# Holding the loads of later batches until the DMA transposes of a batch are done, and issuing the first of those transposes two pairs earlier, in a fused attention and feed-forward kernel

## The chip, the cores and the metric

The kernel runs on one core of one Trainium2 chip. The metric is device time of one execution in microseconds (us). A run is called fast when it is within 1.5% of the fastest of its kernel, and only fast runs are compared. The quoted time is their median. The profile is a trace of one execution; its span is some 2 us shorter than the device time of the same execution (453.2 against 454.95 us for the kernel before), so spans are compared with spans and times with times. In the profile PE is TensorE, PEld its weight loads, DVE VectorE, ACT ScalarE, POOL GpSimd, and SP SyncE; a "q" behind a name means that the line is a DMA issue of that engine.

## The reference

Grouped-query attention (8 batches, 16 query heads, 4 key/value heads, sequence 384, head size 64), and then a feed-forward on the attention's output:

```python
scores = scale * np.matmul(q, k.transpose(0, 1, 3, 2))     # k, v repeated 4 times over heads
attn = softmax(scores)
x = (attn @ v).transpose(0, 2, 1, 3).reshape(B * S, H * D) # 3072 x 1024
h = np.maximum(x @ w_in, 0.0)                              # w_in 1024 x 2048
return (h * h @ w_out).astype(np.float32)                  # w_out 2048 x 1024
```

All inputs and the output are float32 in memory; the kernel computes in bf16.

## The kernel before

A pair is two query heads of one batch: 8 pairs per batch, 64 in all, numbered n. For each pair TensorE computes scores into PSUM, ScalarE takes the exp, TensorE multiplies by v ("attend", one pair behind), and SyncE sends the result through a DMA transpose into `xT` (`put_x`). Between these pieces TensorE works on the feed-forward of the batch before (`fill`), in program order. The feed-forward of batch b may not start before `ready` says so, and it needs `xT` of all 8 pairs of its batch. It begins with the products with `w_in` (the "up matmuls", `f_ps<-xT,w_in_sb` in the profile), in steps of four: the first step of a tile needs `xT` of the batch's first four pairs, the second that of the last four.

q, k and v of a batch are loaded by GpSimd, with a cast from float32 to bf16, into staging buffers (`q_st`, `k_st`, `v_st`). `prepare(b)` then has SyncE transpose k and q by DMA into `kT` and `qT`. Batches 0 and 1 are transposed on TensorE; batch 2 is the first to use `prepare`.

```python
def dup_all_k(b):
    ...                                   # DVE: k_dup <- k_st
    if b + 2 < B:
        load_k(b + 2)

def prepare(b):
    dup_all_k(b)
    R.add("sync", ... dma_start_transpose(kT <- k_dup) ...)
    for part in range(2):
        R.add("sync", ... dma_start_transpose(half of qT <- q_st) ...)
    if b + 2 < B:
        load_q(b + 2)

def prepare_v(b):
    ...                                   # DVE: v_aug <- v_st
    if b + 2 < B and b >= 1:
        load_v(b + 2)
...
for n in range(NPB, NP + 1):              # NPB = 8 pairs of a batch
    per = PER_PAIR[n // NPB]              # ns of feed-forward per pair: 3200 for 8..15, then 5000
    if n < NP:
        scores_pair(n)
    fill(per * 0.4)
    if n > NPB:
        attend(n - 1, 0)
    fill(per * 0.2)
    if n > NPB:
        attend(n - 1, 1)
        put_x(n - 1)
    if n % NPB == (6 if n < 2 * NPB else 4) and n // NPB + 1 < B:
        prepare(n // NPB + 1)
    if n % NPB == 7 and n // NPB + 1 < B:
        prepare_v(n // NPB + 1)
    fill(per * 0.4)
    ready[0] = max(0, n // NPB - 1)
```

Before this loop, the first burst of loads is queued: weights, batches 1 and 2, and, early in the program, q, k and v of batch 3.

The softmax here doesn't subtract the row's maximum and nothing guards it: scores larger than these inputs give would overflow.

Of the kernel before, what the change touches and what calls it, by code (L numbers as in the profile page):

```python
# [106 lines left out]
def bass_gqa_attention__then__ffn_squared_relu_kernel(  # L107
# [11 lines left out]
    B, H, S, D = 8, 16, 384, 64  # L119
# [4 lines left out]
    NPB = H // 2  # L124
# [5 lines left out]
    R = Recorder(nc)  # L130

    def sb(name, shape, dt=bf16):
        return nc.alloc_sbuf_tensor(name, shape, dt)
# [6 lines left out]
    q_st = [sb(f"q_st{i}", [128, H, NJ * D]) for i in range(NST)]  # L140
    k_st = [sb(f"k_st{i}", [128, HKV, NJ, D]) for i in range(NKS)]
    v_st = [sb(f"v_st{i}", [128, HKV, NJ, D]) for i in range(NST)]
# [19 lines left out]
    sc_flat = sc_ps.ap().rearrange("p b c -> p (b c)")  # L162


    def load_k(b):
        st = b % NKS
        R.add("gpsimd", lambda g: g.dma_start(  # L167
            k_st[st].ap().rearrange("p g j d -> p g (j d)"),
            k[b].rearrange("g (p j) d -> p g (j d)", j=NJ)),
            writes=[("k_st", st)], dma=f"k{st}")  # L170

    def load_v(b):
        st = b % NST
        R.add("gpsimd", lambda g: g.dma_start(  # L174
            v_st[st].ap().rearrange("p g j d -> p g (j d)"),
            v[b].rearrange("g (p j) d -> p g (j d)", j=NJ)),
            writes=[("v_st", st)], dma=f"v{st}")

    def load_q(b):
        st = b % NST  # L180
        R.add("gpsimd", lambda g: g.dma_start(  # L181
            q_st[st][:, :, :], q[b].rearrange("h (p j) d -> p h (j d)", j=NJ)),
            writes=[("q_st", st, c) for c in range(NPB)], dma=f"q{st}")

    NWB = 8
    WC = FF // NWB
# [19 lines left out]
    def first_q(c0, c1):  # L206
# [9 lines left out]
        writes=["v_f"], dma="vf")  # L216
# [22 lines left out]
    for c in range(2, NPB):  # L239
        cast_q(c)  # L240
        load_w_in(c - 1)
    load_w_in(7)
    load_k(1)
    load_q(1)
    load_v(1)
    for i in range(2):
        load_w_out(i)
    load_k(2)
    load_q(2)
    load_v(2)  # L250


# [8 lines left out]
    def idle_on_sc(count):  # L261
        def mm(pe):
            for _ in range(count):
                m = pe.matmul(sc_ps[:, 3, 0:256], warm[:, 0:128], warm[:, 0:256])
            return m

        R.add("tensor", mm, reads=["warm"], writes=[("sc", 3)])
# [44 lines left out]
    def dup_all_k(b):  # L312
        src = k_st[b % NKS].ap().rearrange("p g j d -> p (g j) d").unsqueeze(2)
        R.add("vector", lambda e: e.tensor_copy(  # L314
            k_dup[b % 2][:, :, :, :], src.to_broadcast([128, HKV * NJ, 2, D])),
            reads=[("k_st", b % NKS)], writes=[("k_dup", b % 2, g) for g in range(HKV)])
        if b + 2 < B:
            load_k(b + 2)

    def prepare(b):  # L320
        st = b % NST
        dup_all_k(b)
        R.add("sync", lambda e: e.dma_start_transpose(  # L323
            kT[b % 2].ap().rearrange("p g (j c) -> p (g j) c", j=NJ),
            k_dup[b % 2].ap().rearrange("p a x d -> p (a x d)")),
            reads=[("k_dup", b % 2, g) for g in range(HKV)],
            writes=[("kT", b % 2, g) for g in range(HKV)], dma=f"kt{b % 2}")
        for part in range(2):
            cs = range(4 * part, 4 * part + 4)
            R.add("sync", lambda e, cs=cs: e.dma_start_transpose(  # L330
                qT[b % 2][:, cs.start:cs.stop, :].rearrange("p h (t c) -> p (h t) c", t=NJ),
                q_st[st][:, 2 * cs.start:2 * cs.stop, :].rearrange("p h e -> p (h e)")),
                reads=[("q_st", st, c) for c in cs], writes=[("qT", b % 2, c) for c in cs],
                dma=f"qt{b % 2}_{part}")
        if b + 2 < B:
            load_q(b + 2)

    def prepare_v(b):
        R.add("vector", lambda e: e.tensor_copy(
            v_aug[b % 2][:, :, 0:D], v_st[b % NST].ap().rearrange("p g j d -> p (g j) d")),  # L340
            reads=[("v_st", b % NST)], writes=[("v_aug", b % 2)])
        if b + 2 < B and b >= 1:
            load_v(b + 2)

    def operands(p):
# [19 lines left out]
    def scores_pair(p):  # L365
        kt, qt, keys = operands(p)
        half = NJ * S

        def piece(pe, x, j, c0, c1):
            at = x * half + j * S  # L370
            rows = slice(64 * x, 64 * x + 64)
            return pe.matmul(sc_flat[:, at + c0:at + c1], kt[rows, j * 128:(j + 1) * 128], qt[rows, c0:c1])  # L372

        def run(pieces, writes, after=()):
            def mm(pe):
                for pc in pieces:
                    m = piece(pe, *pc)
                return m

            return R.add("tensor", mm, reads=keys, writes=writes, after=after)  # L380

        sc_keys = [("sc", i) for i in range(5)]
        first = run([(0, 2, 256, 384)], sc_keys)
        run([(1, 1, 0, 384), (0, 0, 0, 384), (1, 2, 0, 128), (0, 1, 0, 128), (1, 2, 128, 384),
             (0, 1, 128, 384)], sc_keys)
        run([(1, 0, 0, 384), (0, 2, 0, 256)], sc_keys, after=[first])
        src = sc_flat[:, 0:2 * half].rearrange("p (x a c) -> p x a c", x=2, c=128)
        dst = expT[p % NEX].ap().rearrange("p j (t x c) -> p x (j t) c", x=2, t=NJ)
        R.add("scalar", lambda e: e.activation(dst, src, AF.Exp, scale=0.125),  # L389
              reads=sc_keys, writes=[("expT", p % NEX, j) for j in range(NJ)])  # L390

    def attend(p, s, alone=False):
        b, g = p // NPB, (p % NPB) // 2
        acc, acc_key = (po_alt, ("sc", 1)) if alone and s == 1 else (po_v, "po")

        def av(pe):
            for i in range(NJ):
                f = NJ * s + i
                for j in range(NJ):
                    m = pe.matmul(acc[:, i, s, :], expT[p % NEX][:, j, f * 128:(f + 1) * 128],  # L400
                                  v_aug[b % 2][:, g * NJ + j, :], start=(j == 0), stop=(j == NJ - 1))
            return m

        R.add("tensor", av, reads=[("expT", p % NEX, j) for j in range(NJ)] +
              [("v_aug", b % 2), ("v_one", b % 2)], writes=[acc_key])
        if alone or s == 1:
            ss = slice(s, s + 1) if alone else slice(0, 2)
            w = ss.stop - ss.start
            rinv_v = rinv[p % 2][:, :, ss].unsqueeze(3)
            R.add("vector", lambda e: e.reciprocal(rinv_v, acc[:, :, ss, D:D + 1]),  # L410
                  reads=[acc_key], writes=[("rinv", p % 2)])
            rb = rinv_v.to_broadcast([128, NJ, w, D])
            R.add("vector", lambda e: e.tensor_tensor(o_sb[p % NO][:, :, ss, :], acc[:, :, ss, 0:D], rb, ALU.mult),  # L413
                  reads=[acc_key, ("rinv", p % 2)], writes=[("o_sb", p % NO, s)])

    def put_x(p):
        b, c = p // NPB, p % NPB
        R.add("sync", lambda e: e.dma_start_transpose(
            xT[b % NXT][:, c, :].rearrange("p (i c) -> p i c", i=NJ),
            o_sb[p % NO].ap().rearrange("p i s d -> p (i s d)")),  # L420
            reads=[("o_sb", p % NO, x) for x in range(2)], writes=[("xT", b % NXT, c)], dma=f"xt{p % 8}")
# [71 lines left out]
    def fill(ns):  # L493
        credit[0] += ns
        while credit[0] > 0:
            t = next(ffn, 0)
            if not t:
                credit[0] = 0.0
                return
            credit[0] -= t  # L500
# [32 lines left out]
    idle_on_sc(2)  # L533
    first_oT(NPB - 1, (0,))
    idle_on_sc(3)
    load_q(3)
    fill(6000.0)
    dup_all_k(1)
    fill(1500.0)
    for g in range(HKV):  # L540
        first_kT(g, 1)
        fill(700.0)
    prepare_v(1)
    for c in range(NPB):
        first_qT(c, 1)
        fill(500.0)
    for n in range(NPB, NP + 1):
        per = PER_PAIR[n // NPB]
# [6 lines that stand above are left out]
        if n > NPB:  # L555
            attend(n - 1, 1)
            put_x(n - 1)
        if n % NPB == (6 if n < 2 * NPB else 4) and n // NPB + 1 < B:
            prepare(n // NPB + 1)
        if n % NPB == 7 and n // NPB + 1 < B:  # L560
            prepare_v(n // NPB + 1)
        fill(per * 0.4)
        ready[0] = max(0, n // NPB - 1)
# [32 lines left out]
```

## Time and profile before

| | before |
|---|---|
| time, median of 4 fast runs | 454.34 us (453.99 to 454.69) |
| span of the profile | 453.2 us |
| TensorE busy | 430.9 us |
| longest wait of TensorE | 11.3 us, on the DMA transpose into qT |
| mean granted TensorE clock | 0.981 |

The page of the kernel before: busy time of TensorE, then its busy tenths, the granted clock in tenths and the DMA engines' busy tenths in 40 slices of 11.3 us.

```profile
span 453.2 us, 8216 instructions
...
PE 430.9 (95%) x3591; PEld 241.1 (53%) x3626; DVE 165.7 (37%) x357; ACT 198.8 (44%) x209; POOL 33.2 (7%) x48
...
PE   8989999269999999999999999999999999999997
...
PEclk9999999759999999999999999999999999999999
DMA  9999999960099207921296206121432210220011
```

TensorE is busy nearly throughout, but not in the eighth and ninth slice, 79 to 102 us. There it is busy for 2 and 6 tenths, its clock falls, and the DMA engines are busy for 9 and 6 tenths. The timeline of that stretch (start, duration, engine, line, operation, output<-inputs, count, then the idle time before it and what ended it):

```profile
78.01 0.74 POOL L167 DMA_DIRECT2D k_st<-in_k_dram  x1 [38.71 <-DVE k_dup L314]
78.07 0.67 PE L372 MATMUL sc_ps<-qT,kT 64*128 64x128 bf16 x9
78.49 1.52 SPq L323 DMA_TRANSPOSE kT<-k_dup  x1
78.74 1.17 POOL L181 DMA_DIRECT2D q_st<-in_q_dram  x1
...
79.88 0.78 POOL L174 DMA_DIRECT2D v_st<-in_v_dram  x1
80.05 11.20 SPq L330 DMA_TRANSPOSE qT<-q_st  x2
...
80.97 1.02 PE L447 MATMUL f_ps<-w_out_sb,h2T 128*128 128x512 bf16 x4
...
93.34 1.14 PE L372 MATMUL sc_ps<-qT,kT 64*128 64x128 bf16 x9 [11.35 <-DMA qT<-q_st]
...
97.75 4.68 PE L429 MATMUL f_ps<-xT,w_in_sb 128*128 128x384 bf16 x16
```

The scores of pair 15 start at 78.07, those of pair 16, the first of batch 2, at 93.34. TensorE is idle for 11.35 us because the transposes into `kT` and `qT` were issued at 78.49 and 80.05, in the same two microseconds as the loads of batch 4. The DMA view says how long each took from issue to landing (KB as bf16 in SBUF, us):

```profile
q_st<-in_q_dram POOLq DMA_DIRECT2D x1, 768.0 KB, 13.4
k_st<-in_k_dram POOLq DMA_DIRECT2D x1, 192.0 KB, 5.9
v_st<-in_v_dram POOLq DMA_DIRECT2D x1, 192.0 KB, 13.9
...
kT<-k_dup SPq DMA_TRANSPOSE x1, 8.4
qT<-q_st SPq DMA_TRANSPOSE x1, 13.2
```

13.2 us is the first half of `qT`; the second took 9.6 us. The same transposes of batch 6, which has no load beside it, took 3.9 us (`kT`) and 4.8 and 3.9 us (the halves of `qT`); those of batch 7, without a load too, took 5.6, 5.4 and 4.9 us.

The idle time has a tail. The windows view (stretch, its length, busy us of PE, PEld, DVE, ACT and POOL, then the granted clock, the busy share of the DMA engines and GB/s):

```profile
82.00:84.00 2.00, 0.00 (x0) 0.00 (x0) 0.83 (x2) 0.00 (x0) 0.00 (x0) 1.00 0.47 46
84.00:86.00 2.00, 0.00 (x0) 0.00 (x0) 0.00 (x0) 0.00 (x0) 0.00 (x0) 0.65 1.50 223
...
98.00:100.00 2.00, 2.00 (x8) 0.90 (x7) 0.00 (x0) 1.95 (x1) 0.00 (x0) 0.50 0.03 5
100.00:102.00 2.00, 2.00 (x9) 1.03 (x8) 0.56 (x1) 0.52 (x1) 0.00 (x0) 0.58 0.00 0
```

The clock record of the trace has half clock from 84.60 to 101.67 us, 17.07 us. Between 93.34 and 101.67 TensorE has work again and does it slowly: one pair's scores take 1.14 us where pair 15's took 0.67.

### The profile page before, as it was taken

The numbers are of one execution on the slowest core, as the hardware profiler recorded it, in microseconds if no ns is written. First come the engines' busy times: TensorE is split into PE (matmuls) and PEld (weight loads), VectorE is DVE, ScalarE is ACT, GpSimd is POOL, SyncE is SP. The second block draws the span as 40 slices with busy tenths as digits, with TensorE's granted clock in tenths as the row PEclk, the third lists the DMA queues.
The fourth block names the chain that finished last, engine by engine and source line by source line (L and its number), as shares of the span: only waits on it lengthen the run. The fifth ranks groups of instructions, "written<-read, shape, count | busy, mean of one in ns | idle before, by whom it ended". The sixth has DMA issues, their size and how long they took to land.

```text
span 453.2 us, 8216 instructions
## 1 busy us (share of the span) xinstructions
PE 430.9 (95%) x3591; PEld 241.1 (53%) x3626; DVE 165.7 (37%) x357; ACT 198.8 (44%) x209; POOL 33.2 (7%) x48
## 2 busy tenths in 40 slices
PE   8989999269999999999999999999999999999997
PEld 4556554136655565456655565446654566545543
DVE  3546323114422444324433344234432344214411
ACT  4943654144643465336642466325653266203400
POOL 5931001100010002000200000000000000000000
PEclk9999999759999999999999999999999999999999
DMA  9999999960099207921296206121432210220011
GB/s 245 195 196 204 208 203 164 150 123 19 10 163 174 65 20 99 199 73 42 34 148 165 65 20 124 64 65 56 65 76 88 66 33 17 65 80 23 1 69 70
DMA packets 95939, 44.70 MB, mean 99 GB/s; under 512 B 74400, under 2 KB 89760, under 8 KB 95904
## 3 DMA queue, kind: packets, MB, share of 16 engines
q0 software_dynamic: 34288, 16.65, 28.3%
q1 hardware_dynamic: 59504, 25.96, 25.1%
q10 hardware_dynamic: 2112, 1.57, 1.1%
q8 instruction: 28, 0.46, 0.4%
q14 instruction: 7, 0.06, 0.0%
HBM read 35.65 MB, written 12.58 MB: 106 GB/s over the span
## 4 chain that ended last, share of the span: by engine, by line
PE 91%; DMA 3%; DVE 2%; ACT 2%; issue 1%; SPq 0%
PE f_ps L429 38%; PE f_ps L447 36%; PE po L400 8%; PE sc_ps L372 7%; DMA qT<-q_st 3%; ACT expT L362 1%; PE f_ps L256 1%; PE sc_ps L286 1%; PE sc_ps L356 1%; ACT expT L389 0%; DVE o_sb L413 0%; DVE qT L291 0%; SPq L323 0%; DVE hr L436 0%; DVE y_sb L456 0%
## 5 line engine op out<-in xcount | busy, mean ns | idle before, releaser
L429 PE MATMUL f_ps<-xT,w_in_sb 128*128 128x384 bf16 x1024 | 184.6, 329 | 1.2 <-DVE xT L291 0.7
L447 PE MATMUL f_ps<-w_out_sb,h2T 128*128 128x512 bf16 x733 | 176.0, 379 | 2.0 <-issue 0.2
L389 ACT ACTIVATE expT<-sc_ps 128x2304 bf16<-128x2304 f32 x56 | 116.8, 2085 | 108.8 <-PE sc_ps L372 107.5
L429 PEld LDWEIGHTS f_ps<-xT,w_in_sb 128*128 128x128 bf16 x1024 | 94.1, 98 | 64.2 <-issue 8.0
L438 ACT ACTIVATE h2T<-hr 128x384 bf16<-128x384 f32 x128 | 66.6, 521 | 115.5 <-DVE hr L436 114.2
L447 PEld LDWEIGHTS f_ps<-w_out_sb,h2T 128*128 128x128 bf16 x768 | 68.8, 97 | 75.9 <-issue 5.7
L436 DVE TENSOR_SCALAR hr<-f_ps 128x384 f32<-128x384 f32 x128 | 71.2, 557 | 102.7 <-PE f_ps L429 102.7
L456 DVE COPY y_sb<-f_ps 128x512 f32<-128x512 f32 x48 | 33.2, 691 | 110.6 <-PE f_ps L447 110.2
L400 PEld LDWEIGHTS po<-v_aug,expT 128*128 128x128 bf16 x1143 | 52.1, 98 | 23.8 <-ACT expT L362 2.6
L400 PE MATMUL po<-v_aug,expT 128*128 128x65 bf16 x1143 | 56.9, 194 | 1.3 <-ACT expT L362 0.9
L372 PE MATMUL sc_ps<-qT,kT 64*128 64x128 bf16 (+2 forms) x504 | 38.1, 276 | 12.8 <-DMA qT<-q_st 11.3
L372 PEld LDWEIGHTS sc_ps<-qT,kT 64*128 64x128 bf16 x504 | 21.1, 95 | 34.4 <-issue 28.0
L413 DVE TENSOR_TENSOR o_sb<-po,rinv 128x384 bf16<-128x384 f32 x64 | 35.5, 554 | 2.2
L410 DVE RECIPROCAL rinv<-po 128x6 f32<-128x6 f32 x64 | 12.2, 191 | 55.4 <-PE po L400 55.4
L362 ACT ACTIVATE expT<-sc_ps 128x768 bf16<-128x768 f32 x24 | 18.4, 810 | 4.4 <-PE sc_ps L356 3.6
L167 POOL DMA_DIRECT2D k_st<-in_k_dram x7 | 5.3, 761 | 187.8 <-DVE k_dup L314 187.8
L256 PE MATMUL f_ps<-warm 128*128 128x256 bf16 x29 | 7.2, 360 | 1.5 <-DVE warm L221 1.1
L356 PE MATMUL sc_ps<-qT,kT 64*128 64x384 bf16 x48 | 8.1, 332 | 0.3 <-ACT expT L362 0.2
L181 POOL DMA_DIRECT2D q_st<-in_q_dram x7 | 8.3, 1190 | 0.0
L189 POOL DMA_DIRECT2D w_in_sb<-in_moe_w_in_dram x8 | 7.1, 893 | 0.0
L256 PEld LDWEIGHTS f_ps<-warm 128*128 128x128 bf16 x29 | 3.3, 124 | 4.3 <-DVE qT L291 1.5
L174 POOL DMA_DIRECT2D v_st<-in_v_dram x7 | 5.5, 786 | 0.0
(40 smaller groups left out, 52.3 us busy)
## 6 DMA issues: line engine op xcount, KB each, us to landing
out_dram<-y_sb SPq DMA_DIRECT2D x48, 256.0 KB, 2.0
q_st<-in_q_dram POOLq DMA_DIRECT2D x7, 768.0 KB, 13.4
w_in_sb<-in_moe_w_in_dram POOLq DMA_DIRECT2D x8, 512.0 KB, 10.2
w_out_sb<-in_moe_w_out_dram POOLq DMA_DIRECT2D x2, 2048.0 KB, 32.6
k_st<-in_k_dram POOLq DMA_DIRECT2D x7, 192.0 KB, 5.9
v_st<-in_v_dram POOLq DMA_DIRECT2D x7, 192.0 KB, 13.9
xT<-o_sb SPq DMA_TRANSPOSE x56, 2.3
q_f<-in_q_dram ACTq DMA_DIRECT2D x1, 768.0 KB, 8.6
```

The source lines that it names most:

```text
L256: m = pe.matmul(f_ps[1][:, 0:256], warm[:, 0:128], warm[:, 0:256])
L356: m = pe.matmul(sc_ps[:, 2 * u + x, 0:S], kt[rows, j * 128:(j + 1) * 128], qt[rows, :])
L362: R.add("scalar", lambda e: e.activation(dst, src, AF.Exp, scale=0.125), reads=[("sc", 2 * u), ("sc", 2 * u + 1)], writes=[("expT", p % NE ...
L372: return pe.matmul(sc_flat[:, at + c0:at + c1], kt[rows, j * 128:(j + 1) * 128], qt[rows, c0:c1])
L389: R.add("scalar", lambda e: e.activation(dst, src, AF.Exp, scale=0.125), reads=sc_keys, writes=[("expT", p % NEX, j) for j in range(NJ)])
L400: m = pe.matmul(acc[:, i, s, :], expT[p % NEX][:, j, f * 128:(f + 1) * 128], v_aug[b % 2][:, g * NJ + j, :], start=(j == 0), stop=(j == NJ ...
L413: R.add("vector", lambda e: e.tensor_tensor(o_sb[p % NO][:, :, ss, :], acc[:, :, ss, 0:D], rb, ALU.mult), reads=[acc_key, ("rinv", p % 2)] ...
L429: m = pe.matmul(f_ps[u][:, 0:S], w_in_sb[:, kc, c * 128:(c + 1) * 128], xT[b % NXT][:, kc, :], start=(kc == 0), stop=(kc == NKC - 1))
L436: R.add("vector", lambda e: e.tensor_scalar_max(hr[r][:, :], f_ps[u][:, 0:S], 0.0), reads=[("f_ps", u)], writes=[("hr", r)])
L438: R.add("scalar", lambda e: e.activation(h2T[b % 2][:, c, :], hr[r][:, :], AF.Square), reads=[("hr", r)], writes=[("h2T", b % 2, c)])
L447: m = pe.matmul(f_ps[u][:, :], h2T[b % 2][:, c, i * 128:(i + 1) * 128], w_out_sb[:, c, jj * 512:(jj + 1) * 512], start=(c == 0), stop=(c = ...
L456: R.add("vector", lambda e: e.tensor_copy(y_sb[yb][:, :], f_ps[u][:, :]), reads=[("f_ps", u)], writes=[("y", yb)])
```

## The change

The intent is to keep loads and transposes apart. The loads of batches 3 and on are released by the landing of the last `qT` transpose of batch b-1 or b-2, not by program order (v of batch 4 and later only stands behind the released loads in GpSimd's queue); and the transposes of batch 2 are issued at pair 12 instead of 14, to leave them time before pair 16. The core of the diff:

```diff
-    def load_k(b):
+    def load_k(b, after=()):
...                                        # the same for load_v and load_q; after= adds waits
@@ dup_all_k
-        if b + 2 < B:
-            load_k(b + 2)
@@ prepare
-            R.add("sync", lambda e, cs=cs: e.dma_start_transpose(
+            last = R.add("sync", lambda e, cs=cs: e.dma_start_transpose(
...
-        if b + 2 < B:
-            load_q(b + 2)
+        for ahead in range(b + 1 if b == 2 else b + 2, min(b + 3, B)):
+            load_k(ahead, [last])
+            load_q(ahead, [last])
+            if b == 2 and ahead == 3:
+                load_v(ahead, [last])
@@ prepare_v
-        if b + 2 < B and b >= 1:
+        if b + 2 < B and b >= 2:
             load_v(b + 2)
@@ before the loop
-    load_q(3)
@@ loop
-        if n % NPB == (6 if n < 2 * NPB else 4) and n // NPB + 1 < B:
+        if n % NPB == 4 and n // NPB + 1 < B:
```

More of the change, by code (lines that the diff above doesn't have):

```diff
@@ L169, in load_k, with load_v @@
             k[b].rearrange("g (p j) d -> p g (j d)", j=NJ)),
-            writes=[("k_st", st)], dma=f"k{st}")
-    def load_v(b):
+            writes=[("k_st", st)], dma=f"k{st}", after=after)
+    def load_v(b, after=()):
         st = b % NST
@@ L176, in load_v, with load_q @@
             v[b].rearrange("g (p j) d -> p g (j d)", j=NJ)),
-            writes=[("v_st", st)], dma=f"v{st}")
-    def load_q(b):
+            writes=[("v_st", st)], dma=f"v{st}", after=after)
+    def load_q(b, after=()):
         st = b % NST
@@ L182, in load_q @@
             q_st[st][:, :, :], q[b].rearrange("h (p j) d -> p h (j d)", j=NJ)),
-            writes=[("q_st", st, c) for c in range(NPB)], dma=f"q{st}")
+            writes=[("q_st", st, c) for c in range(NPB)], dma=f"q{st}", after=after)
     NWB = 8
```

## The prediction

> What bounds the kernel now. The page shows TensorE busy 430.9 of 453.2 us; the chain that ended last is 91% TensorE. After the start-up it loses little except in one place. The timeline of 60 to 100 us shows its last matmul of pair 15 ending near 82.0 and the scores of pair 16 (first of batch 2) starting at 93.34, 11.35 us idle, released by the DMA transpose into qT; the chain holds the same step, 13.20 us from 80.05. kT was issued at 78.49, qT at 80.05 (landing after 13.2 and 11.4 us, DMA view), while the loads of batch 4 were issued at 78.0 to 79.9. Batch 6 prepared with no load beside it: kT 3.9 us, qT 4.8 and 4.3 us.
>
> The stall costs more than its length. The windows show the granted clock at 1.00 in 82 to 84, 0.65 in 84 to 86 and 0.50 until about 101.7, some 17.1 us: five of the 3413 ns windows that the Trainium skill gives (TensorE: Matmul & The Clock Gate, Part 1). Work from 93.3 to 102.3 ran cold: scores 1.14 us instead of 0.66, sixteen up matmuls 4.5 instead of 2.6. Estimated loss 2.8 us. Removable: 11.3 + 2.8 = 14.1 us, all on the chain; that alone would give 440.3.
>
> What moves. Batch 3's loads no longer end the first burst: q(3) landed at 72.8, k(3) 74.5, v(3) 76.2. q(2), ahead of them, landed at 65.1 and k(2) at 59.4, so prepare(2) at pair 12 should find its inputs: kT issued near 70.4, qT at 72 to 75.7, landing near 78. Pair 16's scores start near 82: the wait disappears. Work hardly changes.
>
> What it adds. Landing near 78 releases k3, q3, v3, k4, q4, then v4: 2.36 MB in SBUF. The software queue moved 1.95 MB in the 12 us of 54 to 66, so this lasts about 14.5 us, from 79.5 to 94. Feed-forward of batch 1 starts in pair 17, and its second step needs xT of pair 15, issued only near 84.6. Transposes of xT issued under load at 55 to 70 landed in 6.1 to 7.7 us, without load in 2.3. They share engines, as the skill says (DMA: Bandwidth & Descriptors, Issuing engines are not separate DMA queues); the trace agrees. So xT lands near 91.4 while TensorE wants it at 86.25: a new wait of about 5 us, on the chain, in which the clock falls again, about 2 us more (estimate). Before, this wait was 0.28 us. Net: 14.1 - 7.1 = 7.0 us.
>
> Later: windows of 103 to 359 us are over 99% TensorE; transposes of batches 3 to 5 become faster (qT some 10 to 12 us to about 5), which nobody waits for.
>
> Predicted: 447.2 us, 80% range 443.5 to 450. Chances: faster by over 2% 0.25, within 2% 0.73, slower 0.02.
>
> What would show it. No wait of the scores on qT at pair 16; batch 2's kT and qT issued near 70, landed by 80; a new idle time of 4 to 6 us of the up matmuls near 86 to 91, put down to xT's transpose; a second half-clock stretch shorter than 17 us; 103 to 359 as before, shifted.
>
> What would make it wrong. If xT lands in 3 us in spite of the loads, the time falls to 441 to 443. If q(2) lands only after 72, or the transposes take 10 us, part of the first stall stays. If batch 3's loads came too late for pair 20's preparation (near 107), a stall would stand at pair 24; I expect them by 96. The clock window's phase can move 1 to 2 us either way.

## The result

| | before | after |
|---|---|---|
| time, median of 4 fast runs | 454.34 us | 449.31 us (448.15 to 450.41) |
| span of the profile | 453.2 us | 447.2 us |
| longest wait of TensorE | 11.3 us, scores on qT | 7.0 us, up matmuls on xT |
| half clock in that stretch | 17.07 us | 6.83 us |

The ratio is 0.9889, with a 95% interval of 0.9862 to 0.9916: 1.1% faster. A ratio is the mean time of one kernel's fast runs over that of the other's of the same rounds, so it is not quite the ratio of the medians quoted here. In a later set of rounds the same changed kernel gave 450.31 us and 0.9894.

The page of the changed kernel, the same rows:

```profile
span 447.2 us, 8216 instructions
...
PE 428.9 (96%) x3591; PEld 239.7 (54%) x3626; DVE 166.0 (37%) x357; ACT 198.9 (44%) x209; POOL 33.3 (7%) x48
...
PE   7989999579999999999999999999999999999997
...
PEclk9999999979999999999999999999999999999999
DMA  9999997990398108930499206221631200220011
```

The hole in the same place is smaller, not gone. The timeline shows that it is another wait:

```profile
70.40 1.50 SPq L321 DMA_TRANSPOSE kT<-k_dup  x1
...
71.94 3.69 SPq L328 DMA_TRANSPOSE qT<-q_st  x2
...
78.22 0.75 POOL L167 DMA_DIRECT2D k_st<-in_k_dram  x1 [52.98 <-DMA qT<-q_st]
...
81.45 0.66 PE L373 MATMUL sc_ps<-qT,kT 64*128 64x128 bf16 x9
...
83.06 0.56 DVE L414 TENSOR_TENSOR o_sb<-po,rinv 128x384 bf16<-128x384 f32 x1
...
84.90 0.82 PE L430 MATMUL f_ps<-xT,w_in_sb 128*128 128x384 bf16 x4
...
92.70 3.79 PE L430 MATMUL f_ps<-xT,w_in_sb 128*128 128x384 bf16 x12 [6.98 <-DMA xT<-o_sb]
```

The transposes of batch 2 were issued at 70.40, landed by 78.2, and released the loads at 78.22. The scores of pair 16 start at 81.45 without a wait. Then TensorE does the first four up matmuls of batch 1's feed-forward and stands for 6.98 us: the next ones need `xT` of pair 15. SyncE issued that transpose at 84.05; the DMA view of 83.6 to 92 us has its landing:

```profile
q0 software_dynamic: 2402, 0.91, 100.8%
q1 hardware_dynamic: 956, 0.46, 37.5%
...
out_dram<-y_sb SPq DMA_DIRECT2D x1, 256.0 KB, 7.9
xT<-o_sb SPq DMA_TRANSPOSE x1, 8.6
```

8.6 us, where 2.3 us is the usual figure of the whole run. The software queue q0, that of GpSimd's loads, holds only the released loads then. Its packets' time is 100.8% of the sixteen engines' time in the stretch, and that of q1, with the transposes and stores, another 37.5%; the sum is over 100%, so packets of the two overlap. Later stretches did not move: TensorE is busy 47.74 of 48 us and 206.90 of 208 us in 97 to 145 and 145 to 353 us, the same as in 103 to 151 and 151 to 359 us before.

### The profile page after: what moved, and what is told of

It reads as the page before. It is cut to its first block, busy times and chain, and to the rows that moved or that the text cites. A ratio compares the mean times of both kernels' runs of the same rounds, so it can differ in the third digit from the quotient of the medians.

```text
span 447.2 us, 8216 instructions
## 1 busy us (share of the span) xinstructions
PE 428.9 (96%) x3591; PEld 239.7 (54%) x3626; DVE 166.0 (37%) x357; ACT 198.9 (44%) x209; POOL 33.3 (7%) x48
## 3 DMA queue, kind: packets, MB, share of 16 engines
q10 hardware_dynamic: 2112, 1.57, 1.1%
## 4 chain that ended last, share of the span: by engine, by line
PE 93%; DVE 2%; DMA 2%; ACT 1%; issue 1%; SPq 0%
PE f_ps L430 38%; PE f_ps L448 37%; PE po L401 8%; PE sc_ps L373 7%; DMA xT<-o_sb 2%; ACT expT L363 1%; PE f_ps L256 1%; PE sc_ps L286 1%; PE sc_ps L357 1%; DVE o_sb L414 1%; DVE qT L291 0%; DVE hr L437 0%; DVE xT L291 0%; PE f_ps L286 0%; DVE kT L291 0%
## 5 line engine op out<-in xcount | busy, mean ns | idle before, releaser
L373 PE MATMUL sc_ps<-qT,kT 64*128 64x128 bf16 (+2 forms) x504 | 37.2, 271 | 1.9 <-ACT expT L390 1.5
## 6 DMA issues: line engine op xcount, KB each, us to landing
q_st<-in_q_dram POOLq DMA_DIRECT2D x7, 768.0 KB, 12.6
w_in_sb<-in_moe_w_in_dram POOLq DMA_DIRECT2D x8, 512.0 KB, 10.2
```

The source lines that it names most:

```text
L373: return pe.matmul(sc_flat[:, at + c0:at + c1], kt[rows, j * 128:(j + 1) * 128], qt[rows, c0:c1])
```

## The experiments

The theory: loads and transposes share the DMA engines, and the time lost at this place is that of a transpose under load, first `qT`, now `xT` of pair 15. Rival A: only the holding of the loads counts, and moving the transposes does nothing. Rival B: `xT` is late for reasons of SyncE's in-order queue, or is slow at this point by itself. Rival C, for versions that load later still: batch 3 then comes too late for its own preparation. There was also the question of what the clock's fall costs by itself. The runs were made in sets of rounds, on two chips (e1 to e4 on one, e5 to e12 on the other), with the kernel before in each set; across sets the ratios are the safer comparison.

| run | time, us (fast runs) | ratio to before, 95% interval |
|---|---|---|
| e1_move_only | 450.51 (449.86 to 450.96) | 0.9915, 0.9900 to 0.9931 |
| e2_hold_only | 450.71 (448.91 to 452.83) | 0.9929, 0.9904 to 0.9955 |
| e3_both_after_xT | 441.01 (440.44 to 442.02) | 0.9710, 0.9693 to 0.9727 |
| e4_half_after_xT | 449.36 (448.36 to 450.62) | 0.9892, 0.9874 to 0.9910 |
| e5_after_warm | 448.92 (448.10 to 449.78) | 0.9874, 0.9855 to 0.9893 |
| e6_before_warm | 452.96 (452.85 to 453.19) | 0.9964, 0.9946 to 0.9981 |
| e7_fill16 | 438.93 (438.35 to 439.94) | 0.9656, 0.9635 to 0.9677 |
| e8_third_of_b3 | 440.77 (440.42 to 441.08) | 0.9696, 0.9677 to 0.9715 |
| e9_b3_early | 445.05 (441.91 to 446.36) | 0.9782, 0.9753 to 0.9811 |
| e10_after_again | 450.31 (447.20 to 451.61) | 0.9894, 0.9864 to 0.9923 |

All gave correct results. The kernel before gave 454.33 to 454.86 us in these rounds.

### e1: only the earlier transposes

Edit to the kernel before:

```diff
-        if n % NPB == (6 if n < 2 * NPB else 4) and n // NPB + 1 < B:
+        if n % NPB == 4 and n // NPB + 1 < B:
```

> Part one alone: batch 2's transposes at pair 12, loads as in the kernel before (q3 early, k4 and q4 beside the transposes). Theory (loads and transposes share the DMA engines, each new wait is a transpose that met a load): the software queue is full from 66 to about 84, so kT issued at 70.4 and qT at 72 land only near 85, as slowly as before (kT 8 us, qT 11 to 13 us); scores of pair 16 wait about 3 us instead of 11.3; the loads are over by about 84, so xT of pair 15 lands in 2 to 4 us and the up matmuls wait 1 us or less. Time 443 to 446 us. Rival A (holding the loads is what gives the gain): time near the kernel before, 453 to 455. Rival B (xT of pair 15 is late because of the order on the SyncE queue or its own cost there): its wait of about 7 us stays, time 450 or more.

It gave 450.51 us, less of a gain than expected. Its line for the scores of pair 16:

```profile
88.73 1.14 PE L372 MATMUL sc_ps<-qT,kT 64*128 64x128 bf16 x9 [6.93 <-DMA qT<-q_st]
```

The wait is 6.93 us, not 3. `kT`, issued at 70.27, took 11.2 us; the first half of `qT`, for which the scores waited, took 14.5 us and the second 10.7 us. From the issue of `kT` to the start of the scores it is 18.5 us, longer than the 14.9 us before (78.49 to 93.34), while the tail of the first burst and batch 4's loads stood in the queue together: v of batch 4 was issued at 71.44, since GpSimd had nothing to wait for there, and landed 17.4 us later. The up matmuls then had no wait worth the name on `xT`: with the loads over, its transpose landed after 2.4 us. So rival A falls (moving alone gains 3.8 us) and so does rival B's second form (slow by itself); the size of the expected gain was wrong.

### e2: only the held loads

Edit to the changed kernel:

```diff
-        if n % NPB == 4 and n // NPB + 1 < B:
+        if n % NPB == (6 if n < 2 * NPB else 4) and n // NPB + 1 < B:
```

> Part two alone: loads of batches 3 and on held, transposes of batch 2 still at pair 14. Theory: kT issued near 78, no load beside it, last qT lands near 86; scores of pair 16 wait 3.5 to 4.5 us instead of 11.3; the loads are then released near 86, right before xT of pair 15 is issued, which lands in 7 to 9 us, and the up matmuls wait 6 to 8 us: time 451 to 455 us, the gain all given back. Rival A (holding is what gives the gain): time at the changed kernel's 449 or below. Rival B (SyncE order): xT lands as in the changed kernel, too, so this run does not separate it.

It gave 450.71 us, a little better than the 451 to 455 expected; its six runs spread from 448.91 to 452.83 us, and the profiled one (448.95) is among the shortest. `kT`, issued at 78.29, landed after 4.7 us, and the scores waited 2.74 us. The loads were released at 86.72, and `xT` of pair 15 was issued at 87.02. I had expected it to take 7 to 9 us; it took 4.6 us, probably because it left only 0.3 us behind the first load, before the queue had filled. The up matmuls waited 1.77 us. With these two short waits, and one of 1.51 us on the exp between them, the clock was still at half for 10.2 us (86.95 to 97.19). Each half of the change gives some 3.7 us alone, both together 5.0.

### e3: the same loads, released by xT of pair 15

The edit takes the released loads out of `prepare(2)` and puts them behind `put_x(15)`; SyncE's queue keeps its order.

```diff
-        for ahead in range(b + 1 if b == 2 else b + 2, min(b + 3, B)):
+        for ahead in range(b + 2, b + 2 if b == 2 else min(b + 3, B)):
...
-        if b + 2 < B and b >= 2:
+        if b + 2 < B and b >= 3:
             load_v(b + 2)
...
-            put_x(n - 1)
+            last_x = put_x(n - 1)          # put_x now returns the number of its operation
+            if n == 2 * NPB:
+                for ahead in (3, 4):
+                    load_k(ahead, [last_x])
+                    load_q(ahead, [last_x])
+                    load_v(ahead, [last_x])
```

> The changed kernel, with the loads k3, q3, v3, k4, q4, v4 released by the landing of xT of pair 15 instead of qT of batch 2. The SyncE queue keeps its order. Theory: no load in the DMA engines from 67 to 87, xT of pair 15 issued near 84 lands in 2.3 to 3 us, the up matmuls wait 0.5 to 1.3 us instead of 7.0, no half-clock stretch: time 441 to 443 us. The loads then run from 88 to 103, before pair 20's preparation needs batch 3. Rival B (SyncE order or the transposes' own cost): the wait stays at 5 us or more, time 448 or more. Rival C (batch 3's loads come too late): a new wait near pair 24, time above 445.

It gave 441.01 us, 8.3 us below the changed kernel's 449.31, as the theory said. The timeline of the same place:

```profile
83.50 1.18 SPq L419 DMA_TRANSPOSE xT<-o_sb  x1
84.16 0.66 PE L373 MATMUL sc_ps<-qT,kT 64*128 64x128 bf16 x9 [1.51 <-ACT expT L390]
84.75 0.82 PE L430 MATMUL f_ps<-xT,w_in_sb 128*128 128x384 bf16 x4
85.83 2.12 PE L430 MATMUL f_ps<-xT,w_in_sb 128*128 128x384 bf16 x12 [0.25 <-DMA xT<-o_sb]
```

`xT` is issued at nearly the same time (83.50 against 84.05) in the same order on SyncE, and lands after 2.3 us instead of 8.6. The wait is 0.25 us, the twelve matmuls take 2.12 us instead of 3.79, and no half clock is left in the stretch. Nothing but the release of the loads was changed, so they were the cause. The loads now run right behind, and nothing waits for them: TensorE is busy 333.00 of 333 us from 99 to 432 us. Rival C falls as well.

### e4: half the loads held that long

Batch 3's loads are released by `qT` as in the changed kernel, batch 4's by `xT` of pair 15.

```diff
-        for ahead in range(b + 1 if b == 2 else b + 2, min(b + 3, B)):
+        for ahead in range(b + 1 if b == 2 else b + 2, b + 2 if b == 2 else min(b + 3, B)):
...                                        # prepare_v as in e3
+            if n == 2 * NPB:               # against the changed kernel; batch 3 stays in prepare(2)
+                load_k(4, [last_x])
+                load_q(4, [last_x])
+                load_v(4, [last_x])
```

> Half the dose: batch 3's loads released by qT of batch 2 as in the changed kernel, batch 4's by xT of pair 15. Theory: the software queue is busy from 79.5 to about 86.5 instead of to about 97; xT of pair 15 issued near 84 lands near 88 (4 us instead of 8.6), the up matmuls wait about 2.5 us instead of 7.0, and no or one half-clock window: time 442.5 to 445 us, between the changed kernel and the run that releases both later. Rival B: as the changed kernel, 448 or more. If the wait does not depend on the queued amount but only on whether any load is running at issue, it stays near 7 us, time about 449.

A miss: 449.36 us, no better than the changed kernel. The wait is nearly whole:

```profile
85.13 0.82 PE L430 MATMUL f_ps<-xT,w_in_sb 128*128 128x384 bf16 x4
92.53 4.02 PE L430 MATMUL f_ps<-xT,w_in_sb 128*128 128x384 bf16 x12 [6.58 <-DMA xT<-o_sb]
```

The DMA view gives the reason: q of batch 3, issued at 78.56, landed after 11.7 us, and v, issued at 79.70, after 12.6 us, at 92.3 and so just as late as `xT` (92.5). I had reckoned that half of the bytes would be through by 86.5. The rate I had used, 1.95 MB in 12 us, came from a stretch in which the queue was already running; there k, q and v of batch 2 landed within 8.1 us of the load before them (58.4 to 66.5). Here the same 1.18 MB took 14.5 us from the first issue (77.82) to the last landing, of which 4.8 us passed before k, the first, had landed. Half the bytes do not halve a delay when the first half alone outlasts the transpose. By itself this run could also be read in favour of rival B, or as "any load does it"; e8 decides.

### e8: a smaller dose

Only k and v of batch 3 (0.39 MB in SBUF) are released by `qT`; q of batch 3 and all of batch 4 follow `xT` of pair 15.

```diff
...                                        # range and prepare_v as in e4
             load_k(ahead, [last])
-            load_q(ahead, [last])
+            if b != 2:
+                load_q(ahead, [last])
...
             if n == 2 * NPB:               # as in e4, and first
+                load_q(3, [last_x])
                 load_k(4, [last_x])
```

> A smaller dose: qT of batch 2 releases only k3 and v3 (0.39 MB in SBUF); q3 and batch 4 follow xT of pair 15. The run that held only batch 4 gained nothing, as q3 and v3 alone stayed in flight from 79 to 92.7, past xT. Theory: k3 and v3 land by about 84 to 85, when xT of pair 15 is issued, which then lands in 2.3 to 4 us; the up matmuls wait under 1.5 us, no or one half-clock window; time 441 to 443.5 us. Rival (what counts is not which loads are in flight but that the loads start at this point at all, or the SyncE queue): wait of 5 us or more, time 447 or more.

It gave 440.77 us, as much as holding everything.

```profile
85.81 2.12 PE L431 MATMUL f_ps<-xT,w_in_sb 128*128 128x384 bf16 x12 [0.28 <-DMA xT<-o_sb]
```

v of batch 3, issued at 78.18, landed after 5.2 us, by 83.4; `xT` of pair 15 was issued at 83.45 and landed after 2.3 us; the wait was 0.28 us. So it is not the release at this point that hurts, but loads that are still moving when `xT` is. Between e4 and e8 stand q of batch 3 alone and 8.6 us.

### e5 and e6: what the clock costs

Matmuls on zeros fill the wait, so that TensorE does not stand idle: 60 of them in the changed kernel, ahead of the first up matmul of batch 1, and 100 in the kernel before, ahead of the scores of pair 16.

```diff
+        if n == 2 * NPB + 1:               # e5, behind scores_pair(17)
+            idle(60)
+        if n == 2 * NPB:                   # e6, ahead of scores_pair(16)
+            idle(100)
```

> The changed kernel with 60 matmuls on zeros (about 6.5 us) between the scores of pair 17 and the first up matmul of batch 1, so that TensorE is not idle while xT of pair 15 is under way. Measures the clock's share. Theory: no half-clock stretch; the twelve up matmuls after the wait take about 2.0 us instead of 3.8: time shorter by 1.2 to 2.5 us than the changed kernel, 447 to 448. Rival (the clock costs nothing beyond the wait): same time, 449.

> The kernel before with 100 matmuls on zeros (about 10.9 us) ahead of the scores of pair 16, in the 11.3 us in which TensorE waits for qT. Theory: no half-clock stretch from 84.6 to 101.7; scores of pair 16 in 0.66 us instead of 1.14, up matmuls at full speed: shorter by 2.3 to 3.3 us than the kernel before, 451 to 452. Rival (the clock costs nothing beyond the wait): 454.3.

e6 gave 452.96 us, 1.9 us below the 454.86 us of its rounds, the clock staying at 1.000; the expectation was 2.3 to 3.3. The timelines explain the rest: from the start of pair 16's scores to the end of the first two up tiles (the first attend of pair 16) it is 6.51 us (93.66 to 100.17) instead of 8.93 us (93.34 to 102.27), so the half clock cost 2.4 us; but the matmuls on zeros, which began 0.9 us late on another wait, also ran about 0.4 us past the landing of `qT` (93.22; the scores start at 93.66). The rival, that the clock costs nothing, falls for the kernel before.

e5 gave 448.92 us, and it stays inconclusive: the changed kernel gave 449.31 and 450.31 us in two sets of rounds, and the intervals of the ratios overlap. In its profile the twelve matmuls took 2.12 us instead of 3.79 us, so 1.7 us were gained there, but `xT` of pair 15 was also issued later (85.12) and TensorE still waited 1.70 us behind the 60 matmuls.

### e10: the changed kernel once more

No edit.

> The changed kernel once more, to have it in the rounds of the other runs and to see how far one run lies from the next: 448 to 450.5 us, wait of the up matmuls 6 to 8 us.

450.31 us. Its profile, of the longest of the six runs (451.61 us), has a wait of 8.32 us on `xT`, which took 8.8 us from its issue at 86.49. Here SyncE had a share: the output of VectorE that this transpose reads was ready at 84.98, so 1.5 us passed behind a slow issue of the transpose before it (2.98 us) and a store. In the first profile this gap was 0.43 us (83.62 to 84.05). Rival B is thus a small part of the wait, and that part follows from the same load: with the engines free the transposes issue in 1.2 us.

### e9, e11 and e12: batch 3's loads early, batch 4's late

Was it needed at all to move batch 3's loads out of the first burst? Here they stand where the kernel before has them, the transposes of batch 2 are at pair 12, and batch 4's loads follow `xT` of pair 15. Against e3:

```diff
+    load_q(3)
     fill(6000.0)
     dup_all_k(1)
+    load_k(3)
...
     prepare_v(1)
+    load_v(3)
...                                        # behind put_x(15): batch 4 only
```

> Was it needed to move batch 3's loads out of the first burst? Transposes at pair 12, batch 3's loads early as in the kernel before (over by about 77), batch 4's held until xT of pair 15 has landed. Theory: kT and qT of batch 2, issued from 70, share the engines with q3, k3 and v3 until 77 and land near 81 to 84: scores of pair 16 wait 0 to 2.5 us instead of 11.3; xT of pair 15 meets no load, wait below 0.5 us: time 441 to 444.5 us. If batch 3's early loads cost as much as batch 4's did in the run that only moved the transposes (6.9 us of waiting), 447 or more, and the change was right to move them.

The median is 445.05 us, but the six runs go from 441.91 to 446.36, and the profiled one was the fastest of them: no wait on `qT`, 0.24 us on `xT`.

> The run with batch 3's loads early gave 441.9 us in its profiled execution, in which nothing waited, and 444 to 446.4 in the others. A second look at the same kernel. Theory: in the longer executions qT of batch 2 lands after 83, because the first burst ends later or the transposes meet more of it; the scores of pair 16 wait 2 to 4 us and a half-clock stretch follows. Rival: the extra time lies elsewhere, for example in a stretch of low clock without a wait, or at pair 24. If this execution is a short one (442 or less) too, it stays open.

> As the run before it, once more, so that at least one of the two is likely to be a longer execution.

They took 443.93 and 445.20 us (single runs, state unknown). The scores of pair 16 did not wait in either, so my expectation was wrong. The extra time is in the same wait on `xT` as ever, and this time through SyncE's order. From e11:

```profile
74.20 4.92 SPq L328 DMA_TRANSPOSE qT<-q_st  x2
...
83.22 0.58 SPq L460 DMA_DIRECT2D out_dram<-y_sb  x1
83.37 0.56 DVE L414 TENSOR_TENSOR o_sb<-po,rinv 128x384 bf16<-128x384 f32 x1
83.84 1.20 SPq L419 DMA_TRANSPOSE xT<-o_sb  x1
85.08 0.58 SPq L460 DMA_DIRECT2D out_dram<-y_sb  x1
85.70 1.20 SPq L419 DMA_TRANSPOSE xT<-o_sb  x1
88.05 3.40 PE L430 MATMUL f_ps<-xT,w_in_sb 128*128 128x384 bf16 x12 [2.01 <-DMA xT<-o_sb]
```

The tail of the first burst drew out the issue of `kT` and `qT` (8.8 us, 70.32 to 79.12; 5.2 us in the changed kernel, 70.40 to 75.63). The later issues queued behind it, so that `xT` of pair 15, whose input was ready at 83.93, was issued at 85.70; it landed after an undisturbed 2.3 us. A wait of 2.01 us and one window of half clock follow (87.28 to 90.69). So moving batch 3's loads out of the burst was right; what was wrong is the place to which they were moved. e12 shows the same wait (1.88 us). What makes one execution of this version short and another long I have not separated; in e9's profile the issue of the three transposes took 6.8 us.

### e7: the version that beats both

e3, and besides some feed-forward of batch 0 is kept back from pairs 8 to 15 and put where TensorE waits for the exp of pair 16 (1.51 us in e3) and for `xT`.

```diff
-    PER_PAIR = {1: 3200.0, ...}
+    PER_PAIR = {1: 2700.0, ...}
...
+        mid = n != 2 * NPB                 # pair 16: both attends first, then all of the fill
-        fill(per * 0.4)
+        if mid:
+            fill(per * 0.4)
         if n > NPB:
             attend(n - 1, 0)
-        fill(per * 0.2)
+        if mid:
+            fill(per * 0.2)
```

> The run that releases both batches' loads after xT of pair 15, and besides some 3.5 us of feed-forward of batch 0 kept back from pairs 8 to 15 and put behind the second half of attention of pair 15, where TensorE waits for the exp of pair 16 (1.5 us) and xT of pair 15 (about 1 us). Expected: both waits below 0.3 us, time 438.5 to 441 us, 2 to 3 us below the run without it. If the earlier pairs then wait for something else (exp or q of batch 2), less than 1 us is gained.

438.93 us, 3.4% below the kernel before, 2.1 us below e3. The window around the place, first of e7, then of e3; TensorE is busy for 18.00 against 16.24 us out of 18:

```profile
82.00:100.00 18.00, 18.00 (x167) 10.79 (x166) 7.40 (x16) 10.39 (x12) 5.29 (x6) 1.00 1.21 149
...
82.00:100.00 18.00, 16.24 (x157) 9.95 (x157) 7.11 (x16) 11.49 (x12) 5.29 (x6) 1.00 1.07 134
```

## Why the prediction was right

The measured 449.31 us lies in the range of 443.5 to 450, near its upper end, and the class, within 2%, was the likely one. That it fell inside is in part luck: the second set of rounds (e10) gave 450.31 us, just outside. The mechanism was right, and one term of the sum was mis-sized (point 4). Point by point:

1. The removed wait. Right. The scores of pair 16 no longer wait on `qT`; `kT` was issued at 70.40 (predicted 70.4) and all had landed by 78.2 (78). The transposes took 3.8 and 4.2 us.
2. What was removable: 11.3 us of wait and an estimated 2.8 us of slow work, 14.1 us. e6 puts the slow work at 2.4 us. e3, in which both are gone with nothing in their place, is 13.3 us below the kernel before. Right to within a microsecond.
3. The new wait. Right in place, cause and releaser: up matmuls of batch 1, second step, on `xT` of pair 15, under the released loads. e3 shows the cause by removing the loads alone, e8 by leaving a third of batch 3's. What the Trainium skill says (DMA: Bandwidth & Descriptors, Issuing engines are not separate DMA queues), that DMAs of all issuing engines end on the same sixteen and interleave, agrees with what e3 shows: GpSimd's loads slowed SyncE's transpose from 2.3 to 8.6 us. Which part of the path the two compete for, no run here separates.
4. Its size. This is the term that was mis-sized: "xT lands near 91.4 while TensorE wants it at 86.25", about 5 us. It was wanted at 85.72 and came at 92.7, so 7.0 us, and 8.3 us in the second profile. `xT` took 8.6 and 8.8 us, not the 6.1 to 7.7 us of the single transposes at 55 to 70 us; here the transpose of pair 14 and a store were in flight with it. The loads lasted longer, too: "79.5 to 94" was 78.2 (first issue) to 98.7 us (v of batch 4, issued at 82.71, landed 16.0 us later). The rate was taken from a stretch in which the queue was already running; why it was lower here was not separated. e4 failed on this same rate.
5. The second fall of the clock, estimated at 2 us: half clock for 6.83 us, of which TensorE had work in 92.70 to 96.12; half of these 3.4 us, about 1.7 us, were lost (an estimate; e5's profile shows 1.7 us on the twelve matmuls). Near enough.
6. The sum: predicted 14.1 - 7.1 = 7.0 us, measured 5.0 us. With the measured terms, 11.35 + 2.4 - (6.98 - 0.28) - 1.7 = 5.35 us, from the profiles; that agrees with the 5.5 us between the profiles from the scores of pair 15 to the end of the first two up tiles (24.20 us, 78.07 to 102.27, against 18.75 us, 77.58 to 96.33).
7. Later batches: right, TensorE is as full as before; the faster transposes of batches 3 to 5 brought nothing, as nobody waited for them.

## What to carry to other kernels

When a transfer is moved out of one transfer's way, look for the next transfer with a waiter, and release the bulk only behind that one: here the release event alone made 5 us of gain into 13 us. A delay under contention follows from what is still in flight at the moment, not from how many bytes were queued, so half of the loads can cost the whole delay (e4) and a third of that half nothing (e8). A wait of TensorE can also have a price in clock behind it (2.4 us after the wait of 11.35 us, by e6; one window of half clock after 2.01 us in e11), and in an in-order issue queue a slow transpose delays those behind it even after the load is gone (e11).

## What the Trainium skill lacked or had wrong

- TensorE: Matmul & The Clock Gate (Part 1, and the table "Why this matters for your kernels") says that half clock comes after at least one idle window of about 3.4 us, and to avoid idle gaps over about 3 us. Here it came with smaller gaps. In e11 the clock fell at 87.28 after a stretch of 3.41 us in which TensorE was busy 1.42 us, and no gap inside it was longer than 1.3 us; the whole wait was 2.01 us. In e2 it fell at 86.95 after 3.41 us with 1.34 us busy, and in the kernel before at 84.60, 2.6 us after the last matmul. (A later section of Part 1 says that frequent short idles can throttle too, but gives no length or share for it.) The length of the half-clock stretches agrees with the page: 17.07, 10.24, 6.83 and 3.41 us are 5, 3, 2 and 1 of its 3413 ns windows.
- DMA: Bandwidth & Descriptors (Anatomy of one DMA) gives 2.0 us and bytes over 436 GB/s for a software-queue transfer. The q load of one batch, 0.79 MB in SBUF and 1.57 MB in memory, would take 3.8 or 5.6 us by that; it took 8.3 us in e8 (q of batch 3, nothing ahead of it in the queue, the loads of batch 4 behind it), and up to 18.8 us in e5 (q of batch 4), with other loads ahead and transposes beside it. So the formula is too short for this load; the page's table of measured transfers, with 6.15 us for 1 MB, is longer than the formula too. The page has no figure for loads that cast from float32 to bf16 in such short rows.
- The pages have bandwidths for DMA transposes, but no time for a small one within SBUF on this chip, alone or under load. Here one of 128x384 bf16 took 2.3 us alone and 4.6 (e2) to 9.7 us (e5) beside the software queue's loads, and its issue on SyncE 1.2 us alone and up to 2.98 us (e10) under load.
